# The output weights of the first six heads split by partitions into loads of 112, 5, 5, 5 and 1

## The chip, the core and the metric

The kernel runs on one core of one Trainium2 chip. The metric is the device time of one execution in microseconds (us), lower is better. The engines are TensorE (PE in the profile, with its weight loads as PEld), VectorE (DVE), ScalarE (ACT), GpSimd (POOL) and SyncE (SP). Transfers run on the core's sixteen DMA engines, whichever queue issues them.

## The reference

One decode step of grouped-query attention over a cached context, gated by a small feed-forward network. There are 2 sequences, 32 query heads, 8 key and value heads, a context of 32,768, a head size of 128 and a model width of 512; everything is float32.

```python
xn = _layernorm(x)                                   # x: 2 x 1 x 512
q = (xn @ wq).reshape(B, Sq, 32, 128)
scores = jnp.einsum("bhqd,bhkd->bhqk", q, k) * (128 ** -0.5)
o = jnp.einsum("bhqk,bhkd->bhqd", softmax(scores), v)
s = o.reshape(B, Sq, 4096) @ wo                      # wo: 4096 x 512
h = relu(xn @ w1 + b1) ** 2
g = silu(h @ w2 + b2)
out = x + s * g
```

The two caches hold 512 MB between them; the weights `wo` are 8 MB.

## The kernel before

The kernel is a stream of large loads with the computation behind it. All loads of the stream are issued on SP by `load` (line 163) into two buffers of SBUF, `slot0` and `slot1`, of 64 KB a partition, 8 MB in all. The order is: the query weights, the two feed-forward weights in one load, then for each of the 16 pairs of sequence and key head two loads of keys and two of values. SP waits with each load until TensorE has finished with the buffer's last contents; `release` gives a buffer free and issues the next load of the list `todo`.

Every load has 128 partitions, and its source in memory is laid out by the host (`packed`, line 456), so that what goes into one partition is contiguous.

For each pair the scores are computed with keys as the moving operand in four groups of 32 columns, then a common maximum, exponentials (ScalarE), transposes of the probabilities, and the products with the values. These steps stand in a loop of 16 rounds that TensorE, ScalarE and VectorE run. The result of a pair goes into `oT`, transposed, and its last step is the VectorE product at line 393.

The output weights lie in a buffer of their own, `wo_sb`, of 32 heads x 512 x 4 bytes a partition. They are loaded at the end of the stream: when the last value load has been issued, `release` issues on SP at once, without a wait, a load for each entry of `PIECES` (line 184) and then two loads of 64 rows by 512 for the halves of the last head (line 187). A piece of `n` heads puts `n` x 2,048 bytes into each of 128 partitions. Each has a semaphore of its own, `piece_sem`.

After the loop TensorE multiplies by the output weights, head by head: for each piece it waits for the piece's semaphore (line 415) and then takes its heads. The first 27 heads are products of 512 columns into `wb`; the last five are split over the four groups of columns (`narrow`). What `wb` holds is copied by ScalarE (line 423) and folded into `acc` by eight small products once head 29 is done. Two VectorE steps (lines 439 and 441) apply the gate and add `x`, and SP writes the output (line 443).

Two more loads matter for reading the profile. ScalarE's queue issues a load of 22 rows (`small`, line 202) and two loads of 8 rows each (`xb`, line 205) at the very start, all of rows of 512 bytes.

Of the kernel before, what the change touches and what calls it, by code (L numbers as in the profile page):

```python
# [15 lines left out]
P = 128  # L16
B, D, HQ, HKV, SK, DH, F = 2, 512, 32, 8, 32768, 128, 1792
# [8 lines left out]
FJ = FG // 32  # L26
SLOT = HALF
NSLOT = 2
PIECES = (16, 8, 4, 2, 1)
WIDE = 27  # L30
HN = P // 2
SCALE = 1.0 / math.sqrt(DH)
# [92 lines left out]
def build(nc, x22, x8, kt, vt, wq, wm, wo, out):  # L125
    pe, act, dve = (Looped(nc, e, n) for e, n in ((nc.tensor, "pe"), (nc.scalar, "act"), (nc.vector, "dve")))
    pool, sp = (Engine(nc, e, n) for e, n in ((nc.gpsimd, "pool"), (nc.sync, "sp")))

    def mm(*args, **kw):
        pe.do("matmul", *args, **kw)  # L130
# [4 lines left out]
    def sb(name, *shape):  # L135
        return nc.alloc_sbuf_tensor(name, [P, *shape], F32)

    slots = [sb(f"slot{i}", SLOT) for i in range(NSLOT)]
    wo_sb = sb("wo_sb", HQ * D)
# [16 lines left out]
    slot_sem = [nc.alloc_semaphore(f"slot{i}") for i in range(NSLOT)]  # L156
    piece_sem = [nc.alloc_semaphore(f"piece{i}") for i in range(len(PIECES) + 2)]
    small_sem, xe_sem, out_sem = (nc.alloc_semaphore(n) for n in ("small", "xe", "out"))
# [4 lines left out]
    def load(src, width):  # L163
        i = issued[0] % NSLOT
        issued[0] += 1
        if free[i] is not None:
            sp.wait(free[i])
        count[i] += 16
        nc.sync.dma_start(slots[i][:, 0:width], src).then_inc(slot_sem[i], 16)  # L169
        return i, (slot_sem[i], count[i])  # L170
# [6 lines left out]
    def release(token):  # L177
        free[stream.pop(0)[0]] = token
        if todo:
            stream.append(load(*todo.pop(0)))  # L180
            if not todo:
                h = 0
                for n, sem in zip(PIECES, piece_sem):
                    nc.sync.dma_start(wo_sb[:, h * D:(h + n) * D], wo[h * P:(h + n) * P].rearrange("(p h) e -> p (h e)", h=n)).then_inc(sem, 16)
                    h += n
                for u in range(2):
                    nc.sync.dma_start(wo_sb[:, h * D + u * NG * HN:h * D + (u + 1) * NG * HN],
                                      wo[h * P + u * HN:h * P + (u + 1) * HN].rearrange("r (t e) -> (r t) e", t=2)).then_inc(piece_sem[len(PIECES) + u], 16)

# [62 lines left out]
    for d in range(ND):  # L252
        for f in range(2):
            for c in range(NG):
                lo = d * HQ * DH + (f * NG + c) * W
                mm(sc[f][32 * c:32 * c + 32, :], xT[:, d, :], slots[i][:, lo:lo + W], start=(d == 0), stop=(d == ND - 1))
    t = pe.done()
    release(t)
    act.wait(t)
    t_q = [act.done("copy", prob[:, f, :], sc[f][:, :]) for f in range(2)]  # L260
# [19 lines left out]
    def scores(u):  # L280
        i, t = stream[0]
        pe.wait(t, t_set, t_exp[u])
        for j in range(NJ):
            for c in range(NG):
                lo = (c * NJ + j) * W
                mm(sc[u][32 * c:32 * c + 32, :], qz[:, 28 - 4 * j:60 - 4 * j], slots[i][:, lo:lo + W],
                         start=(j == 0), stop=(j == NJ - 1))
        t = pe.done()
        release(t)
        dve.wait(t)  # L290
        return t, dve.done("tensor_reduce", rm[:, u:u + 1], sc[u][:, :], axis=AX.X, op=ALU.max)

    def mlp():
# [18 lines left out]
        for j in range(FJ):  # L312
            c = j % NG
            lo = FJ * D + j * D
            mm(wb[32 * c:32 * c + 32, :], hT[:, j, :], slots[i][:, lo:lo + D], start=(j < NG), stop=(j >= FJ - NG))
        t = pe.done()
        release(t)
        act.wait(t)
        t = act.done("copy", o_sb[:, :], wb[:, :])
# [16 lines left out]
    for s in range(NS):  # L336
        for e in (pe, act, dve):
            e.starts.append(len(e.ops))
        hkv, b = divmod(s, B)
# [32 lines left out]
        for u in range(2):  # L372
            i, t = stream[0]
            pe.wait(t, t_pT[u], t_osb)
            for n in range(32):
                y = n % NG
                k, r = divmod(n, 8)
                lo = k * 32 + r * 4
# [7 lines left out]
        for n in range(4):  # L386
            lo = n * (P - REP)
# [11 lines left out]
    def heads(h, u):  # L399
        hkv, k = divmod(h, REP)  # L400
        lo = 2 * hkv * REP * 16 + (1 - u) * REP + k
        return oT[:, lo:lo + 31 * REP + 1:REP]
# [3 lines left out]
    h = 0  # L406
# [3 lines left out]
    def narrow(h, u, los, stop):  # L410
        for c in range(NG):
            mm(acc[32 * c:32 * c + 32, :HN], heads(h, u), wt[:, h, los[c]:los[c] + HN], start=(h == WIDE and u == 0), stop=stop)

    for n, sem in zip(PIECES, piece_sem):
        pe.wait((sem, 16))
        for h in range(h, h + n):
            if h < WIDE:
                c = h % NG
                mm(wb[32 * c:32 * c + 32, :], heads(h, 0), wt[:, h, :], start=(h < NG), stop=(h >= WIDE - NG))
                if h == WIDE - 1:  # L420
                    t = pe.done()
                    act.wait(t, t_otr)
                    t_w = act.done("copy", o_sb[:, :], wb[:, :])
                continue
            for u in range(2):
                narrow(h, u, [c * P + u * HN for c in range(NG)], False)
            if h == WIDE + 2:
                pe.wait(t_w)
                for u in range(2):
                    for c in range(NG):  # L430
                        lo = c * P + u * HN
                        mm(acc[32 * c:32 * c + 32, :HN], selg[:, 32 - u:64 - u], o_sb[:, lo:lo + HN], start=False, stop=False)
        h += 1
    for u in range(2):
        pe.wait((piece_sem[len(PIECES) + u], 16))
        narrow(h, u, [(u * NG + c) * HN for c in range(NG)], u == 1)
# [19 lines left out]
def packed(A_x, A_k_cache, A_v_cache, A_wq, A_wo, B_w1, B_b1, B_w2, B_b2):  # L456
# [11 lines left out]
    parts, h = [], 0  # L468
    for n in PIECES:
        parts.append(w[h:h + n].transpose(1, 0, 2).reshape(n * P, D))  # L470
# [25 lines left out]
```

## Time and profile before

| what | value |
|---|---|
| median of three runs | 1303.53 us (1303.4 to 1303.53) |
| span of the profiled execution | 1301.8 us |
| DMA queue of SP, share of 16 engines | 99.7% |
| mean rate over the span | 431 GB/s, 561 MB |
| TensorE busy | 672.3 us, 52% |
| VectorE, ScalarE, GpSimd busy | 49.5, 78.9 and 5.4 us |

The page gives the profiled execution's span, from its first instruction to its last, and the three times are of whole executions. All engines but the DMA engines have long idle times; which of them end the run has to be read from its last stretch, in which the loads run out. The rows of a table by stretches give the share of the sixteen DMA engines that are busy, so that 0.25 is four engines. The profile's DMA rows count packets by queue: q1 is SP's, q10 is ScalarE's, and the rows called "instruction" are fetches of code. A packet of the stream is what one engine moves in one piece, up to 65,536 bytes.

### The profile page before, as it was taken

Reading aid. Unit: us, or ns where it says so; the run is one execution under the profiler, and the core shown is the slowest. Engines: PE = TensorE matmul, PEld = TensorE weight load, DVE = VectorE, ACT = ScalarE, POOL = GpSimd, SP = SyncE. Lnnn points to the kernel's source line nnn. Section 1 sums busy time; section 2 is a strip of 40 time slices with the busy share of each in tenths; the row PEclk is TensorE's granted clock in tenths of the full one; section 3 lists DMA queues with packets and bytes.
Section 4 is the critical chain, followed back from the end, with each engine's and each line's share of the span. In section 5 each row is a group of like instructions: output and inputs, shape, how many; then the busy total and the mean of one; then the engine's idle time right before and its main releaser. Section 6 shows DMA issues by size and latency. Waiting matters only on the chain.

```text
span 1301.8 us, 10286 instructions
## 1 busy us (share of the span) xinstructions
PE 672.3 (52%) x4671; PEld 208.2 (16%) x4671; DVE 49.5 (4%) x166; ACT 78.9 (6%) x138; POOL 5.4 (0%) x29
## 2 busy tenths in 40 slices
PE   3456455535546545545635544554554654554565
PEld 1111111201112111111212111111111211111122
DVE  0000000000000000000000000000000000000000
ACT  1010010100001010010101001010010101001010
POOL 0000000000000000000000000000000000000000
PEclk9776667677677778677767767767767767767778
DMA  9999999999999999999999999999999999999998
GB/s 406 433 446 423 445 423 447 419 441 429 429 441 427 443 425 445 423 447 419 439 431 427 443 427 443 425 445 421 447 421 439 431 427 443 427 443 425 445 421 362
DMA packets 10726, 561.13 MB, mean 431 GB/s; under 512 B 1339, under 2 KB 1633, under 8 KB 1889
## 3 DMA queue, kind: packets, MB, share of 16 engines
q1 hardware_dynamic: 10656, 561.03, 99.7%
q8 instruction: 5, 0.08, 0.0%
q10 hardware_dynamic: 65, 0.02, 0.0%
HBM read 561.01 MB, written 0.03 MB: 431 GB/s over the span
## 4 chain that ended last, share of the span: by engine, by line
DMA 75%; PE 24%; issue 1%; DVE 0%; ACT 0%; SPq 0%; DVEq 0%; ACTq 0%
DMA slot<-in_vt 36%; DMA slot<-in_kt 36%; PE sc L63 12%; PE o_ps L63 11%; DMA slot<-in_wm 3%; PE wb L63 1%; DVE hT L63 0%; PE ot L63 0%; DVE o_sb L63 0%; ACT o_sb L63 0%; DVE yb L63 0%; SPq L169 0%; DVE t L63 0%; DVE oT L63 0%; DVEq L101 0%
## 5 line engine op out<-in xcount | busy, mean ns | idle before, releaser
L63 PE MATMUL sc<-slot,qz 128*32 128x512 f32 x2048 | 295.3, 741 | 300.0 <-DMA slot<-in_kt 300.0
L63 PE MATMUL o_ps<-slot,pT 128*16 128x512 f32 x2048 | 294.3, 739 | 208.9 <-DMA slot<-in_vt 208.9
L63 PEld LDWEIGHTS sc<-slot,qz 128*32 128x32 f32 x2048 | 81.1, 133 | 503.4 <-issue 503.4
L63 PEld LDWEIGHTS o_ps<-slot,pT 128*16 128x16 f32 x2048 | 69.3, 113 | 420.6 <-issue 420.6
L63 ACT ACT_TABLE_LOAD x19 | 24.4, 1283 | 650.5 <-DVE nm L63 647.6
L63 PE MATMUL tp<-ident,prob 128*128 128x128 f32 x136 | 31.0, 397 | 53.3 <-ACT prob L63 53.2
L63 DVE TENSOR_REDUCE rm<-sc 128x1 f32<-128x512 f32 x32 | 22.1, 692 | 575.1 <-PE sc L63 575.1
L63 ACT COPY o_sb<-o_ps 128x512 f32<-128x512 f32 x16 | 9.4, 585 | 504.7 <-PE o_ps L63 504.7
L63 PEld LDWEIGHTS tp<-ident,prob 128*128 128x128 f32 x136 | 23.8, 204 | 57.9 <-issue 56.1
L63 DVE TENSOR_REDUCE t<-ot 128x4 f32<-128x64 f32 x16 | 3.6, 224 | 524.0 <-PE ot L63 524.0
L63 ACT ACTIVATE prob<-sc,nm 128x512 f32<-128x512 f32 x32 | 21.7, 682 | 0.2
L63 ACT COPY pT<-tp 128x512 f32<-128x512 f32 x32 | 18.7, 585 | 13.8 <-PE tp L63 13.8
L63 PE MATMUL sc<-slot,xT 128*32 128x512 f32 x64 | 8.4, 684 | 17.5 <-DMA slot<-in_wq 17.5
L63 PE MATMUL ot<-ident,o_sb 128*128 128x128 f32 x64 | 10.1, 280 | 13.7 <-ACT o_sb L63 13.7
L63 PEld LDWEIGHTS ms<-selh,l 128*128 128x128 f32 x64 | 15.6, 334 | 0.0
L63 PE MATMUL ms<-ident,r 128*128 128x128 f32 x16 | 4.7, 294 | 20.0 <-DVE r L63 20.0
L63 PE MATMUL ms<-selh,l 128*128 128x4 f32 x64 | 13.7, 319 | 0.0
L63 PEld LDWEIGHTS ot<-ident,o_sb 128*128 128x128 f32 x64 | 6.7, 141 | 27.9 <-issue 27.9
L63 PE MATMUL wb<-slot,xT 128*32 128x448 f32 x32 | 4.6, 738 | 6.6 <-DMA slot<-in_wm 6.6
L273 POOL COPY qz<-qT 128x4 f32<-128x4 f32 x16 | 3.0, 186 | 1167.3 <-PE sc L63 1137.3
L63 PEld LDWEIGHTS ms<-ident,r 128*128 128x128 f32 x16 | 2.1, 133 | 34.1 <-issue 34.1
L63 PE MATMUL wb<-wo_sb,oT 128*32 128x512 f32 x54 | 6.2, 596 | 0.7 <-DVE oT L63 0.7
(62 smaller groups left out, 55.6 us busy)
## 6 DMA issues: line engine op xcount, KB each, us to landing
slot<-in_wm SPq DMA_DIRECT2D x1, 7168.0 KB, 38.3
wo_sb<-in_wo SPq DMA_DIRECT2D x1, 4096.0 KB, 39.3
wo_sb<-in_wo SPq DMA_DIRECT2D x1, 2048.0 KB, 43.7
wo_sb<-in_wo SPq DMA_DIRECT2D x1, 1024.0 KB, 45.8
slot<-in_kt SPq DMA_DIRECT2D x32, 29.2
slot<-in_vt SPq DMA_DIRECT2D x32, 29.2
wo_sb<-in_wo SPq DMA_DIRECT2D x1, 512.0 KB, 46.6
wo_sb<-in_wo SPq DMA_DIRECT2D x1, 256.0 KB, 46.7
```

The source lines that it names most:

```text
L63: instruction = getattr(self.e, name)(*[x(i) if callable(x) else x for x in args], **kw)
L273: return pool.done(g.tensor_copy(qz[:, 28:32], qT[:, b, hkv, :]))
```

## The change

The first piece, of 16 heads, becomes two: one of 6 heads and one of 10. The piece of 10 heads is loaded as before, by one load of 128 partitions. The piece of 6 heads is loaded by five loads, by partitions: 0 to 111, 112 to 116, 117 to 121, 122 to 126, and 127. The last is written as 16 parts of 192 numbers. All five count on the same semaphore, and TensorE waits for 5 x 16 before head 0 in place of 16. The host lays out `wo` by the new pieces. The later pieces, the last head's two halves and all instructions of the computation stay.

```diff
-PIECES = (16, 8, 4, 2, 1)
+PIECES = (6, 10, 8, 4, 2, 1)
+UNEVEN = ((0, 112), (112, 117), (117, 122), (122, 127), (127, 128))
...
                 for n, sem in zip(PIECES, piece_sem):
-                    nc.sync.dma_start(wo_sb[:, h * D:(h + n) * D], wo[h * P:(h + n) * P].rearrange("(p h) e -> p (h e)", h=n)).then_inc(sem, 16)
+                    to, of = wo_sb[:, h * D:(h + n) * D], wo[h * P:(h + n) * P].rearrange("(p h) e -> p (h e)", h=n)
+                    for lo, hi in (UNEVEN if h == 0 else [(0, P)]):
+                        a, b = to[lo:hi], of[lo:hi]
+                        if hi - lo == 1:
+                            a, b = (x.rearrange("p (a b) -> p a b", a=16) for x in (a, b))
+                        nc.sync.dma_start(a, b).then_inc(sem, 16)
                     h += n
...
     for n, sem in zip(PIECES, piece_sem):
-        pe.wait((sem, 16))
+        pe.wait((sem, 16 * len(UNEVEN) if h == 0 else 16))
```

## The prediction

> **What bounds the kernel now.** I read the page's span and chain first, then the last 50 us of the chain in order of time, then the DMA share in short stretches, and last the DMA packets by queue.
>
> ```profile
> span 1301.8 us, 10286 instructions
> ...
> DMA 75%; PE 24%; issue 1%; DVE 0%; ACT 0%; SPq 0%; DVEq 0%; ACTq 0%
> ```
>
> The span is 1301.8 us; the median of the three runs is 1303.53, so 1.7 us lie around the span. I work out differences on the span and add them to the median. The rule for "same" is 0.2%, which is 2.6 us here and about what a measurement of this kernel can tell from no change.
>
> Three quarters of the chain are DMA. The next fence is a table of stretches (start:end, length, busy time of PE, PEld, DVE, ACT, POOL with counts, clock, share of the 16 DMA engines, GB/s):
>
> ```profile
> 60.00:1250.00 1190.00, 622.46 (x4223) 190.07 (x4223) 41.75 (x137) 67.27 (x120) 2.79 (x15) 0.73 1.00 434
> ...
> 1297.00:1297.20 0.20, 0.20 (x9) 0.10 (x5) 0.00 (x0) 0.00 (x0) 0.00 (x0) 1.00 0.70 231
> 1297.20:1297.40 0.20, 0.20 (x7) 0.08 (x3) 0.00 (x0) 0.00 (x0) 0.00 (x0) 1.00 0.33 123
> ...
> 1297.40:1298.60 1.20, 1.20 (x52) 0.88 (x46) 0.00 (x0) 0.59 (x1) 0.00 (x0) 1.00 0.26 95
> 1298.60:1298.90 0.30, 0.30 (x34) 0.30 (x28) 0.00 (x0) 0.00 (x0) 0.00 (x0) 1.00 0.09 31
> 1298.90:1299.20 0.30, 0.30 (x34) 0.30 (x24) 0.00 (x0) 0.00 (x0) 0.00 (x0) 1.00 0.00 0
> ```
>
> The first row says that all sixteen DMA engines are busy all the time at 434 GB/s, or 27.1 GB/s each. That makes a row of 6 heads (6 x 512 x 4 = 12,288 bytes) 0.45 us on one engine. The other rows say that they do not finish together: from 1297.4 to 1298.6 the share is 0.26, which is four engines of sixteen, and these end between 1298.6 and 1298.9. Twelve engines are done about 1.4 us before the last four. So the end of the weight loads is set by four engines, and the change moves work between engines.
>
> Behind the last bytes stands little:
>
> ```profile
> 1279.87 9.64 PE o_ps L63 x64
> ...
> 1291.68 5.50 PE wb L63 x49
> ...
> 1297.92 1.84 PE sc L63 x89
> 1299.76 0.02 issue
> 1299.78 0.23 DVE yb L63
> ...
> PEld wb L63 <- DMA wo_sb<-in_wo: 0.6, 1, 0.6
> ```
>
> The chain is put on TensorE from 1279.87 on: the last value product, then the output weights. In the last 12 us the only wait for `wo_sb` is the last row, 0.6 us of a weight load, and the rows above show TensorE busy up to 1299.76. So weights that come earlier gain at most that 0.6 us, and weights that come more than about 0.6 us later move the end one for one. This is the asymmetry of the case.
>
> **Which engines are late.** The queue of instruction fetches:
>
> ```profile
> q1 hardware_dynamic: 10512, 560.99, 99.9%
> q8 instruction: 4, 0.07, 0.0%
> q10 hardware_dynamic: 65, 0.02, 0.0%
> ...
> q8 instruction: 1, 0.02, 62.1%
> ```
>
> Up to 1299 us there are four instruction packets (packets, MB, share of 16 engines). The last row is the one in the stretch 44.0 to 44.1: 62.1% of 16 x 0.1 us, or 0.99 us. The others start near 55.97, 89.65 and 126.0. An engine that serves one falls behind and stays behind, because its queue is never empty. Four packets, four late engines.
>
> Which four? An engine's packets follow each other without a gap, so the chains can be followed back by their times. The fetches of 55.97 and 89.65 sit on engines that also carry the two 8-row loads of `xb`; the other two do not.
>
> ```profile
> q10 hardware_dynamic: 3, 0.00, 2.2%
> ...
> q10 hardware_dynamic: 8, 0.00, 1.9%
> ...
> q1 hardware_dynamic: 3, 0.20, 3245.5%
> ...
> q1 hardware_dynamic: 5, 0.33, 3332.1%
> ```
>
> The first two rows count small packets from 7.2 us to 7.428 and to 7.9: eight engines take part, and the one with the fetch of 89.65 is third. The last two count the first packets of `wq` from 1.79 us to 1.808 and to 1.820: the chain with the fetch of 89.65 is third to start, the one with the fetch of 55.97 fifth. The 65 packets of q10 are 22 + 8 + 8 = 38 rows and 27 completions, and 27 = 11 + 8 + 8: a load of 22 rows runs on 11 engines and a load of 8 on 8, the same 8 both times. If queues start in the order of engines, a load of 5 rows runs on the first five, and two of the late engines, the third and the fifth, are among them.
>
> **The change part by part.** On SP, the queue that issues the loads, before and now:
>
> ```order
> L169 DMA slot<-in_vt 128x16384 x2
> L184 DMA wo_sb<-in_wo 128x8192
> L184 DMA wo_sb<-in_wo 128x4096
> L184 DMA wo_sb<-in_wo 128x2048
> L184 DMA wo_sb<-in_wo 128x1024
> ```
>
> This is the end of SP's program before, from the last value loads (`slot`) into the weights (`wo_sb`).
>
> ```order
> L170 DMA slot<-in_vt 128x16384 x2
> L190 DMA wo_sb<-in_wo 112x3072
> L190 DMA wo_sb<-in_wo 5x3072 x3
> L190 DMA wo_sb<-in_wo 1x3072
> L190 DMA wo_sb<-in_wo 128x5120
> L190 DMA wo_sb<-in_wo 128x4096
> ```
>
> One load of 16 heads has become six; nothing else has moved, and TensorE, VectorE and ScalarE run the same instructions.
>
> *Five more issues.*
>
> ```profile
> 1250.03 2.33 SPq L184 DMA_DIRECT2D wo_sb<-in_wo  x5
> 1252.42 0.90 SPq L187 DMA_DIRECT2D wo_sb<-in_wo  x2
> ...
> wo_sb<-in_wo SPq DMA_DIRECT2D x1, 4096.0 KB, 39.3
> ```
>
> 2.33 / 5 = 0.47 us each, so 2.3 us more, ending near 1255.6 instead of 1253.3. The first weight bytes land 39.3 us after 1250.03; the queued value loads cover it, and SP's next instruction, the output, comes at 1300. Cost nothing.
>
> *The new wait.* TensorE now waits for five loads before head 0 and for one before head 6. Both used to be one landing at 1250.03 + 39.3 = 1289.3, which is 2.4 us before TensorE starts on the weights at 1291.68. Cost nothing by itself.
>
> *Bytes per engine.* Before: 8 rows of 32,768 = 262,144. Now every engine has 7 rows of 12,288, a sixteenth of the single row (768) and 8 rows of 20,480 = 250,624, which is 11,520 less, or -0.43 us. The first five also have three rows of 12,288: 287,488, which is 25,344 more, or +0.94 us. Eleven more packets add little:
>
> ```profile
> DMA packets 27, 0.40 MB, mean 3084 GB/s; under 512 B 6, under 2 KB 21, under 8 KB 21
> ...
> q10 hardware_dynamic: 21, 0.01, 21.3%
> ```
>
> From 1.70 to 1.83 us the 21 packets of q10 are 15 rows of 512 bytes and 6 completions. 21.3% of 16 x 0.13 us = 0.44 us, so about 26 ns a row at most, against 19 ns by 27.1 GB/s: some 7 ns for a packet, 0.08 us for eleven. So a late engine among the first five ends 1.0 us later, less the up to 0.3 us by which it may not have been the very last: +0.9 us.
>
> *Several engines on the same partitions.* In a load of 128 partitions each engine fills 8 of its own. The three loads of 5 send five engines into partitions 112 to 126 at the same time, while the two owners of these sixteen partitions stream into them too. The trace has no such case at this size. The lower bound is nothing: the 26 ns rows just shown are two rows an engine into neighbouring partitions, unstretched. The upper one is that what one engine now brings in, 27.1 GB/s, is all that eight partitions take. By it the first load of five shares with the owner, six streams, and a row lasts 6 x 0.45 = 2.7 us (+2.3); of the second, three rows and the owner, +1.4; the third is like the first, +2.3: together +5.9. Where the early engines have passed when the late two come, three streams share and each of the three rows costs +0.9, together +2.7. The 112-partition load hands out 7 neighbouring rows an engine, which no longer fit eights; a shared row costs 0.45, none to all seven of them: 0 to 3.2. [...] For the loads of five I take the middle of 2.7 and 5.9, 4.3; for the 112 one row of seven, 0.5.
>
> Sum: 0.9 + 4.3 + 0.5 = +5.7 us on the last landing. TensorE, idle by then, passes it on: 1303.53 + 5.7 = 1309.2.
>
> [...]
>
> **Rivals.** *No sharing.* The 512-byte rows speak for it. Then +0.9: 1304.4, within 0.2%.
>
> *The first five are all early, and nothing is shared.* Then the late four lose 0.43 us, the first five (+1.0) stay behind the 1.4 us lead, and the end comes 0.0 to 0.4 earlier: 1303.3. This is the case on the other side; it decides if neither late chain is among the first five. Against it stand the third and fifth place above.
>
> [...]
>
> *The first five are early, with sharing.* 5.7 less 1.4 of lead: +4.3, 1307.8.
>
> *A load of 5 rows runs on one engine,* so that the split isn't what the code says. Fifteen rows of 0.45 us more on one engine, less one: +6.4, less 1.4 if it is early: +5.0, 1308.5. The 27 completions speak against it.
>
> **How the numbers follow.** Sharing with a late engine among the five: 0.6. No sharing, late engine: 0.24. All early, no sharing: 0.07. All early, sharing: 0.06. One engine: 0.03. Slower by over 0.2% is the first and the last two, less a little for sharing that stays under 2.6 us: 0.67. Faster by over 0.2% has no case, since at most 0.6 us can be won; 0.01. Same: 0.32. Range of the likeliest: from 0.9 + 2.7 to 0.9 + 5.9 + 1.0, 1307.1 to 1311.3. The range of the whole reaches down to the unshared case: 1304.0 to 1311.3.
>
> **What would show it.** Sharing: from 1280 to 1295 us the GB/s fall well under 434 while the DMA share stays near 1, and the chain before the last products is DMA `wo_sb`. No sharing: full rate, and the stretch with a low DMA share grows by 0.9 us with two engines in it at the end. I am wrong if TensorE still has no wait for `wo_sb` over 0.6 us, or if the last weight bytes land before 1299.3.

## The result, and the profile after

The changed kernel takes 1309.86 us (median of five runs, 1309.4 to 1310.25) against 1303.53 us before (1303.4 to 1303.59): 6.3 us more, a ratio of 1.0048 with a 95% interval of 1.0037 to 1.006. The profiled execution has a span of 1308.1 us, also 6.3 more than before.

The page of the changed kernel: span, packets of SP's queue, chain.

```profile
span 1308.1 us, 10291 instructions
...
q1 hardware_dynamic: 10816, 561.03, 99.7%
...
DMA 76%; PE 23%; issue 1%; SPq 0%; DVE 0%
DMA slot<-in_kt 36%; DMA slot<-in_vt 34%; PE sc L64 11%; PE o_ps L64 10%; DMA wo_sb<-in_wo 4%; DMA slot<-in_wm 3%; PE wb L64 1%; SPq L190 0%; DVE hT L64 0%; SPq L170 0%; DVE o_sb L64 0%; DVE yb L64 0%; SPq L174 0%
```

The weights are on the chain now (4%). Before, the page's chain had no weights in it:

```profile
DMA slot<-in_vt 36%; DMA slot<-in_kt 36%; PE sc L63 12%; PE o_ps L63 11%; DMA slot<-in_wm 3%; PE wb L63 1%; DVE hT L63 0%; PE ot L63 0%; DVE o_sb L63 0%; ACT o_sb L63 0%; DVE yb L63 0%; SPq L169 0%; DVE t L63 0%; DVE oT L63 0%; DVEq L101 0%
```

Where the time goes is seen in stretches at the end of the stream. The last three columns are TensorE's clock, the share of the sixteen DMA engines that are busy, and GB/s; a packet counts whole in the stretch in which it starts, so that a share can pass 1. The kernel before:

```profile
1277.00:1279.00 2.00, 0.00 (x0) 0.00 (x0) 0.00 (x0) 0.00 (x0) 0.00 (x0) 0.50 0.99 426
1279.00:1283.00 4.00, 3.13 (x16) 0.76 (x20) 0.00 (x0) 0.00 (x0) 0.00 (x0) 0.50 0.95 410
1283.00:1287.00 4.00, 4.00 (x32) 1.04 (x28) 0.00 (x0) 0.00 (x0) 0.00 (x0) 0.75 0.93 401
1287.00:1291.00 4.00, 3.10 (x28) 0.91 (x20) 0.00 (x0) 0.58 (x1) 0.00 (x0) 1.00 1.01 430
```

The changed kernel:

```profile
60.00:1250.00 1190.00, 614.21 (x4223) 188.53 (x4223) 41.47 (x136) 67.34 (x120) 2.82 (x15) 0.74 1.00 434
...
1277.00:1279.00 2.00, 0.00 (x0) 0.00 (x0) 0.00 (x0) 0.00 (x0) 0.00 (x0) 0.50 0.83 209
1279.00:1283.00 4.00, 1.45 (x8) 0.37 (x12) 0.00 (x0) 0.00 (x0) 0.00 (x0) 0.50 0.94 205
1283.00:1287.00 4.00, 4.00 (x24) 0.96 (x20) 0.00 (x0) 0.00 (x0) 0.00 (x0) 0.51 1.06 168
1287.00:1291.00 4.00, 4.00 (x40) 0.95 (x32) 0.00 (x0) 0.00 (x0) 0.00 (x0) 1.00 0.97 351
1291.00:1295.00 4.00, 2.41 (x20) 0.92 (x16) 0.39 (x2) 0.59 (x1) 0.00 (x0) 1.00 0.96 409
```

From 1279 to 1287 all sixteen engines are busy as before (a share of 0.94 and 1.06, against 0.95 and 0.93), but they move 205 and 168 GB/s where 410 and 401 were moved before. They are not waiting for work; their packets last longer: the rows of 12,288 bytes take from 460 to 1,572 ns in this trace (median 884), and in the run below that loads the same piece with one load, 460 to 473 ns. Against the kernel before, the four stretches from 1277 to 1291 lack 0.43, 0.82, 0.93 and 0.32 MB. That is 2.5 MB, 5.8 us of the stream, of the 6.3 us.

TensorE then waits for the weights, which before cost it 0.6 us:

```profile
PEld wb L64 <- DMA wo_sb<-in_wo: 5.7, 3, 3.0
PE wb L64 <- DMA wo_sb<-in_wo: 3.0, 3, 2.1
```

The chain in order of time now ends through the load of the piece of 4 heads (start, duration, what):

```profile
1253.63 49.49 DMA wo_sb<-in_wo
...
1303.65 0.60 PE wb L64 x3
1304.25 1.85 PE sc L64 x90
1306.11 0.02 issue
1306.13 0.23 DVE yb L64
```

From there on it is the tail of before, 6.3 us later: the last small products start at 1304.25 where they started at 1297.92.

The last value product starts late as well, which the prediction had not said:

```profile
1281.55 9.68 PE L64 MATMUL o_ps<-slot,pT 128*16 128x512 f32 x64 [11.11 <-DMA slot<-in_vt]
```

Before it started at 1279.87. The values were queued ahead of the weights. But engines that are 1.4 us ahead are already writing weights while the late ones still write values, and the values of the late ones are slowed: a packet of 65,536 bytes of values takes 2.42 us before, and the four that start last, from 1276.28 to 1276.72, take 3.35 to 3.84 us in this trace.

### The profile page after: what moved, and what is told of

Same layout as the page of the kernel before. It is cut to its first block, busy times and chain, and to the rows that moved or that the text cites. A ratio compares the mean times of both kernels' runs of the same rounds, so it can differ in the third digit from the quotient of the medians.

```text
span 1308.1 us, 10291 instructions
## 1 busy us (share of the span) xinstructions
PE 670.4 (51%) x4671; PEld 207.4 (16%) x4671; DVE 49.4 (4%) x166; ACT 79.0 (6%) x138; POOL 5.4 (0%) x29
## 3 DMA queue, kind: packets, MB, share of 16 engines
q1 hardware_dynamic: 10816, 561.03, 99.7%
## 4 chain that ended last, share of the span: by engine, by line
DMA 76%; PE 23%; issue 1%; SPq 0%; DVE 0%
DMA slot<-in_kt 36%; DMA slot<-in_vt 34%; PE sc L64 11%; PE o_ps L64 10%; DMA wo_sb<-in_wo 4%; DMA slot<-in_wm 3%; PE wb L64 1%; SPq L190 0%; DVE hT L64 0%; SPq L170 0%; DVE o_sb L64 0%; DVE yb L64 0%; SPq L174 0%
## 5 line engine op out<-in xcount | busy, mean ns | idle before, releaser
L64 PE MATMUL sc<-slot,qz 128*32 128x512 f32 x2048 | 291.3, 733 | 300.3 <-DMA slot<-in_kt 300.3
L64 PE MATMUL o_ps<-slot,pT 128*16 128x512 f32 x2048 | 291.3, 733 | 214.4 <-DMA slot<-in_vt 214.4
```

Source lines behind the costliest of these rows:

```text
L64: instruction = getattr(self.e, name)(*[x(i) if callable(x) else x for x in args], **kw)
```

## The experiments

Two theories stood against each other. By the first, engines that write into neighbouring partitions at the same time share what such a set of partitions takes, so that the cost lies in where the rows go. By the second, there is no sharing, and only the bytes of each engine and its lead or lag count. All medians below are compared with runs of the kernel before on the same chip (1303.46, 1303.45 and 1303.56 us).

### The cut into 6 and 10 heads alone

```diff
-UNEVEN = ((0, 112), (112, 117), (117, 122), (122, 127), (127, 128))
+UNEVEN = ((0, 128),)
```

> The piece of 6 heads as one load of 128 partitions; the pieces are 6, 10, 8, 4, 2, 1 as in the changed kernel. If the split by partitions is what costs, this gives the time of before back: +0.1 us for the eight packets and the one completion more that each engine has. If the new cut into 6 and 10 heads, or the waits for them, were the cost, the +6.3 us of the change would stay.

Measured: 1303.07 us (1302.91 to 1303.15, ten runs), 0.4 us less than before (ratio 0.9996, 0.9987 to 1.0006). In the same stretches of its trace the rate stays up:

```profile
1279.00:1283.00 4.00, 3.29 (x16) 0.75 (x20) 0.00 (x0) 0.00 (x0) 0.00 (x0) 0.50 1.01 429
1283.00:1287.00 4.00, 4.00 (x36) 1.09 (x32) 0.00 (x0) 0.00 (x0) 0.00 (x0) 0.83 1.01 432
```

So the whole cost is in the split by partitions, none in the new pieces. This version has the lowest median of all. Its ten times lie below the 31 times of the kernel before beside it (1303.23 to 1304.1), though the interval of the ratio includes 1; why it should be 0.4 us faster stays open.

### Five engines, with the places of the rows changed

The kernel before, with three loads of 5 rows of 10,240 bytes into an unused buffer, once four partitions apart and once side by side:

```diff
+    spare = sb("spare", 5 * D)
...
+                    if h == 0:
+                        for lo, hi, step in SPARE:
+                            n_rows = len(range(lo, hi, step))
+                            nc.sync.dma_start(spare[lo:hi:step, :], wo[0:5 * n_rows].rearrange("(p h) e -> p (h e)", h=5)).then_inc(spare_sem, 16)
...
+SPARE = ((0, 17, 4), (1, 18, 4), (2, 19, 4))
...
+SPARE = ((112, 117, 1), (117, 122, 1), (122, 127, 1))
...
-    sp.wait(t)
+    sp.wait(t, (spare_sem, 16 * len(SPARE)))
```

> The kernel before, with three further loads of 5 partitions (10,240 bytes each) into an unused buffer, behind the piece of 16 heads. Their partitions lie four apart (0, 4, 8, 12, 16 and so on), so that as few as can be fall into one set. 3 x 0.38 = 1.1 us of bytes more for each of five engines. [...] If all five are early, the 1.4 us of lead hides it: 0.

> As the run with partitions four apart, and the same bytes on the same five engines, but the three loads go to partitions 112 to 116, 117 to 121 and 122 to 126 of the unused buffer, as in the changed kernel. No sharing: the same time as that run, +1.1 us or 0. Sharing among neighbours: +4.2 us with eights, as an estimate by following the engines row by row. [...]

Measured: 1303.13 us four apart (-0.3), 1306.05 us side by side (+2.6; ratio 1.002, 1.0011 to 1.003). The same bytes on the same five engines, and 2.9 us between them. The size written down for sharing, +4.2, was too large. Both traces, the four apart first, in the stretch in which the rows go in:

```profile
1286.90:1288.30 1.40, 1.40 (x17) 0.37 (x13) 0.00 (x0) 0.00 (x0) 0.00 (x0) 1.00 1.08 458
1288.30:1291.30 3.00, 1.67 (x16) 0.53 (x8) 0.23 (x1) 0.58 (x1) 0.00 (x0) 1.00 1.01 429
```

```profile
1286.90:1288.30 1.40, 1.40 (x16) 0.35 (x12) 0.00 (x0) 0.00 (x0) 0.00 (x0) 1.00 1.37 222
1288.30:1291.30 3.00, 1.27 (x12) 0.42 (x4) 0.39 (x2) 0.59 (x1) 0.00 (x0) 1.00 0.79 155
```

This shows the sharing by itself: 429 GB/s against 155 at a time when only the partitions differ, and 438 against 176 over both stretches together. The rows of 10,240 bytes take 385 to 392 ns in the first trace, and 385 to 1,567 ns (median 1,034) in the second. Partitions 112 to 126 are not slow by themselves: the one load of 128 fills them too, and none of its rows takes over 473 ns. The theory without sharing falls.

The run four apart shows something else. It cost nothing, so that all five engines had the lead to hide 1.1 us in. The tail of its trace says the same:

```profile
1297.80:1298.00 0.20, 0.20 (x17) 0.12 (x7) 0.00 (x0) 0.12 (x1) 0.00 (x0) 1.00 0.63 225
```

At 1298 the share is 0.63, some nine or ten engines, where before it was 0.26, four. The five with the extra rows have joined the four late ones; had two of the late been among the five, there would have been seven. The prediction had put two late engines among them.

### Where the late engines are

> The same with six rows a load, the first six engines. If the sixth is one of the late two, +1.1 us; if the two are the seventh and the eighth, the same time as with five rows.

> As the run with five rows four partitions apart, but eight rows a load: 1.1 us of bytes more on the first eight engines, three of which that run did not touch. The chains of the prediction put two late engines among these eight. With five of them early and untouched in their place, the two must be among the three new ones: the end +1.1 us, and the last pieces land on six early engines as before, not on four. If no late engine is among the eight, the time stays that of the run with five.

The edit, against the run with five rows four apart:

```diff
-SPARE = ((0, 17, 4), (1, 18, 4), (2, 19, 4))
+SPARE = ((0, 21, 4), (1, 22, 4), (2, 23, 4))
...
+SPARE = ((0, 29, 4), (1, 30, 4), (2, 31, 4))
```

Measured: 1303.46 us with six (1302.97 to 1304.27, -0.1) and 1303.94 us with eight (1303.22 to 1304.23, +0.4). The medians are not what was written down for a late engine, +1.1. The profiled executions, both with a span of 1302.6 us, tell more. Six rows a load first, then eight, at the very end of the loads:

```profile
1299.20:1299.50 0.30, 0.30 (x33) 0.30 (x25) 0.00 (x0) 0.22 (x1) 0.00 (x0) 1.00 0.07 24
```

```profile
1299.20:1299.50 0.30, 0.30 (x33) 0.30 (x28) 0.00 (x0) 0.11 (x1) 0.00 (x0) 1.00 0.14 48
```

0.07 of sixteen is one engine, 0.14 is two: after 1298.9, where the kernel before is done, one late engine still has extra work with six rows a load, and two with eight. So in these executions one late engine was the sixth and another the seventh or eighth; with the run of five, none was among the first five. The packets of 10,240 bytes agree. Each engine has three; the last of them starts by 1288.44 on all five engines of the run of five, by 1288.72 on five of the six and at 1289.34 on the other, by 1288.70 on six of the eight and at 1289.21 and 1289.26 on the other two. The ten times with six rows fall into two groups, five at 1303.0 to 1303.1 and five at 1303.8 to 1304.3. The ten with eight rows do the same, three at 1303.2 to 1303.4 and seven at 1303.9 to 1304.2. Both profiles are of the upper groups. Most likely such an engine is late in some executions and not in others, which a single profile can't show.

### The 112 without the rest

```diff
-UNEVEN = ((0, 112), (112, 117), (117, 122), (122, 127), (127, 128))
+UNEVEN = ((0, 112),)
...
+                sp.wait(t_wo)
...
+    t_wo = pool.done(g.memset(wo_sb[:, 0:6 * D], 0.0))
```

> Of the five loads of the first piece only that of 112 partitions is left; partitions 112 to 127 of these six heads are filled with zeros beforehand, so the result leaves those weights out. The prediction put most of the cost into the loads of 5: with them gone, its terms leave 0.5 us for the 112 less 0.4 us for the missing row of each engine, about +0.1 us. Without any sharing it is -0.4 us by bytes, of which TensorE's own pace lets at most 0.1 to 0.2 through, so 0 to -0.2. If neighbouring runs of 7 rows an engine collide all the way, up to 3.2 less 0.4 by the prediction's bound: +2.8 us. Following every engine row by row with 27.1 GB/s for each eight partitions, engines waiting in line, gives +6.1 as an estimate. [...]

Measured: 1306.51 us, +3.05 (1305.66 to 1307.84; ratio 1.0024, 1.0015 to 1.0034). The prediction had 0.5 for this load, and the cost is also above the +2.8 written down for neighbours that collide all the way. The ten times fall into two groups, five at 1305.7 to 1306.2 and five at 1306.9 to 1307.8, so that the median lies between them; the profile is of the upper group. Its trace:

```profile
1279.00:1283.00 4.00, 1.62 (x8) 0.37 (x12) 0.00 (x0) 0.00 (x0) 0.00 (x0) 0.50 0.94 215
1283.00:1287.00 4.00, 4.00 (x36) 1.10 (x32) 0.00 (x0) 0.00 (x0) 0.00 (x0) 0.81 1.03 292
```

The load of 112 partitions alone halves the rate in the first of these stretches. So half of the cost of the change lies in the load that looks most like an ordinary one.

### 112 and 16, with even bytes

```diff
+UNEVEN = ((0, 112), (112, 128))
```

> The piece of 6 heads as loads of 112 and 16 partitions: 7 rows and 1 row an engine, so that every engine moves the bytes that it moved before, none more. No sharing: +0.1 us. Sharing: the cost of the 112 and of sixteen engines in the last sixteen partitions; with eights +6.3 as an estimate by following the engines row by row. [...]

Measured: 1308.52 us, +5.07 (ratio 1.0039, 1.0024 to 1.0053). Here no engine has more bytes to move than before, and still most of the 6.3 us are there. The estimate by eights, +6.3, was 1.2 us too much.

### Halves and quarters

The line for halves, then the line for quarters:

```diff
+UNEVEN = ((0, 64), (64, 128))
...
+UNEVEN = ((0, 32), (32, 64), (64, 96), (96, 128))
```

> The piece of 6 heads as two loads of 64 partitions, 4 rows an engine each; every engine moves the bytes that it moved before. No sharing: +0.1 us. Sharing: two engines in each set of partitions at all times, so that each of the eight rows takes 0.45 us more, 8 x 0.45 = +3.6 us, with sets of eight neighbours or with other sets of eight.

> The piece of 6 heads as four loads of 32 partitions, 2 rows an engine each. No sharing: +0.1 us. If eight neighbours share, four engines meet in each set: 8 x 3 x 0.45 = up to +11 us, +9.7 as an estimate by following the engines row by row with their leads. [...]

Measured: 1309.98 us with halves, +6.5 (ratio 1.005, 1.0034 to 1.0067), and 1309.48 us with quarters, +6.0 (1.0045, 1.0028 to 1.0062). Quarters cost no more than halves. With sets of eight neighbours four engines would meet in quarters and two in halves, and quarters would cost much more (+9.7 by the estimate written down); that form of the theory falls. The traces, halves first and then quarters:

```profile
1280.00:1284.00 4.00, 1.72 (x12) 0.43 (x16) 0.00 (x0) 0.00 (x0) 0.00 (x0) 0.50 0.96 200
```

```profile
1280.00:1284.00 4.00, 1.22 (x8) 0.36 (x12) 0.00 (x0) 0.00 (x0) 0.00 (x0) 0.50 0.98 194
```

About half the rate of before in both (200 and 194 GB/s, where the kernel before moved 410 and 401 from 1279 to 1287), as it would be if two engines met in each set both times. Which partitions then form a set is not shown.

The size for halves was too small: 3.6 us expected and 6.5 measured. A part of it is seen: the last value product starts at 1282.28 in the trace of halves.

```profile
1282.28 9.76 PE L64 MATMUL o_ps<-slot,pT 128*16 128x512 f32 x64 [13.12 <-DMA slot<-in_vt]
```

That is 2.4 us after 1279.87, so the late engines lose time on their values before their weights begin (the last four packets of values take 3.8 to 4.6 us there in place of 2.42), which the working of 3.6 did not count. That this is the whole difference isn't shown.

### One head in place of six

```diff
-PIECES = (6, 10, 8, 4, 2, 1)
+PIECES = (1, 15, 8, 4, 2, 1)
```

> The changed kernel's five loads, but for one head (2,048 bytes a partition) with a second piece of 15 heads. The same number of loads, issues and completions, a sixth of the bytes. If the cost goes with the bytes that share or are moved, 6.3 / 6 = about +1.0 to +1.5 us. If it is a cost of each load or of issuing, +6.3 us stays.

Measured: 1304.1 us, +0.65 (1303.77 to 1304.21; ratio 1.0004, 0.9995 to 1.0014). The same loads with a sixth of the bytes cost about a tenth, less than the +1.0 to +1.5 written down. So it is no price of a load, an issue or a completion.

## Why the prediction was right, point by point

The forecast was 1309.2 us, +5.7, slower by sharing; 1309.86 came out, +6.3. That engines which write into neighbouring partitions slow each other is shown (155 GB/s side by side, 429 four apart), but all three terms of the sum were off (0.9, 4.3 and 0.5 where the runs give about 0, 3.5 and 3.05), and the total is near because their errors offset each other. That is luck.

- *TensorE gains nothing from early weights and passes late ones on.* The second half is borne out: with the weights late, the wait of its weight loads for them grew from 0.6 to 5.7 us, and the end moved by 6.3. No run here brought the weights much earlier.
- *The bytes on a late engine, +0.9.* Wrong: about 0, by the run four apart. The step that failed is "if queues start in the order of engines". That two late engines are among those of the 8-row loads agrees with the profile of the run with eight rows; but the third and fifth place in starting was not an engine's number here. They were among the sixth to eighth, and the five had lead enough.
- *Sharing in the loads of 5, +4.3.* Right in kind, too large. That rows of 12,288 bytes share, where the rows of 512 bytes (26 ns at most) showed nothing of it, was my guess, and no run had shown it; side by side, rows of 10,240 bytes took a median of 1,034 ns where 385 to 392 was the time four apart. The two runs with three loads of 5 differ by 2.9 us with rows of 10,240 bytes, which is an estimate of 2.9 x 12,288 / 10,240 = 3.5 for the rows of the change.
- *Sharing in the load of 112, +0.5.* Mis-sized, and the largest error: 3.05 measured alone, between two groups of times. I had taken one shared row of seven an engine; it was near the upper bound, 3.2. That run moves one row of 0.45 us less on each engine, so that the sharing in it is about 3.5 as an estimate, above that bound. Why it is so much is not shown; the bound left out that the values ahead of the load are slowed too (the last value product starts at 1281.38 in that run, 1.5 us late).
- *The sum.* 3.05, which has the missing row in it, and 3.5 make 6.5, against 6.3 measured. The two parts were measured in different kernels, so that they need not add up exactly.
- *The sets.* I used eights of neighbours for the price; quarters and halves show that they are not eights (+6.0 and +6.5 us, where eights gave +9.7 and +3.6). What the sets are instead is not shown; the traces do not name the engine or the partition of a packet.
- *A sixteenth of the single row for each engine.* Wrong: SP's packets went from 10656 to 10816, 160 more. These are 128 rows and 32 completions (16 for the piece of 10, 5 for each load of 5 and 1 for the single row). In sixteenths it would have been 190. The row went to one engine as one packet: the trace has 128 packets of 12,288 bytes, 112 and 15 and this one.
- *Five more issues cost nothing.* Borne out in time, not in form. They were said to end near 1255.6; the last two took 15 us:

```profile
1255.43 15.05 SPq L193 DMA_DIRECT2D wo_sb<-in_wo  x2
```

The last of them was held until 1270.5. The kernel with the piece of 6 in one load has the same hold, until 1271.6, and loses no time by it:

```profile
1254.18 17.39 SPq L193 DMA_DIRECT2D wo_sb<-in_wo  x2
```

- *What would show it.* The rate well under 434 GB/s at a DMA share near 1 came up to 1291, and `wo_sb` on the chain came as written.
- *The rivals.* No sharing (+0.9) is excluded by the runs four apart and side by side, and with it the case of early engines without sharing. A load of 5 rows on one engine is excluded by the 160 packets: with one completion for each load of 5 there would be 148. "Early, with sharing" is what happened, as far as the run four apart tells of the changed kernel; it had 0.06 and was priced at 1307.8, where the likeliest case had 0.6. The forecast of the time was better than its reasons.

## What to carry to other kernels

In these runs, with a load of 112 partitions, or loads of 64 or of 32, ahead of full loads of 128, all DMA engines looked busy from 1279 to 1287 us (a share of 0.91 to 1.12) while the rate was 168 to 292 GB/s; with full loads alone it was 401 to 432. Several engines in the same set of partitions at a time is the explanation that the loads of 5 bear out (155 GB/s side by side, 429 four apart). A few uneven rows meant to use 1.4 us of idle engines cost 6.3 us here, and a load of 112 partitions alone cost 3.05. Before moving work to engines that end early, see what the end is worth (here at most 0.6 us), and try loads of 128 partitions, or rows some partitions apart, first: the piece of 6 heads in one load took 1303.07 us, and the rows four apart 1303.13, against 1303.46 before.

## What the runs showed of the hardware that was not expected

- With a load of 112 partitions at the head of the weights the stretches ran at 215 and 292 GB/s, and with one of 128 at 429 and 432; a row of 12,288 bytes took 476 to 1,191 ns in place of 460 to 473.
- In the changed kernel and with halves the loads queued behind the values slowed them: the last values landed so much later that the product on them started 1.7 us later in the changed kernel and 2.4 us later with halves. In the run with the loads of 5 side by side the full load of 16 heads lies between, and the product starts at 1279.89, as before.
- In the changed kernel and with one load of 128 for the piece of 6, SP's issue of the last load was held 14.7 and 16.9 us (0.9 us for both last issues before); nothing waited for it here. The number of loads does not decide it: the run with the 112 alone has as many loads as the one with 128, and its last two issues took 0.43 us each. What does decide it is not shown.
- Which engines are late differs between executions, as far as the two groups of times with six rows a load tell (five at 1303.0 to 1303.1 and five at 1303.8 to 1304.3).
